# First MoE's first layer of an attention and two-MoE kernel: from fp32r pairs to scaled fp16 pairs, with TensorE's order in the attention stage fixed to the order of the code

## The chip, the cores and the metric

One core of a Trainium2 chip runs the whole program. The metric is the device time of one execution in microseconds (us), the median over runs.

## What is computed

Causal attention over 4 batches x 8 heads x 576 tokens x 64 dims with a bias from a running sum, then two MoE layers without routing, each `x @ w_in`, a gate, and `@ w_out`, over 2304 tokens (512 wide, 2048 inside). The weights come as float64, 8 bytes a number.

```python
bias = -(cum[:, :, :, None] - cum[:, :, None, :])           # cum: running sum of max(s, 0)
scores = where(causal, -1e9, scale * q @ k.T + minimum(bias, 0.0))
attn = exp(scores - scores.max(-1)); attn = attn / (attn.sum(-1) + 1e-9)
x = (attn @ v) as [2304, 512]
h = x @ w_in;  g = h * tanh(log1p(exp(h)));  x = g @ w_out          # first MoE
h = x @ w2_in; g = h / (1 + exp(-1.702 * h)); out = g @ w2_out      # second MoE
```

## The kernel before

**Attention.** It is cut into `steps` (26 a batch, 104 in all): one step is 128 query rows of one to four heads (64 rows of two heads in the last tile of a batch). `tick` emits one step: `do_qk` (tile `s` in PSUM: scores, then a mask matmul), `do_max` (VectorE adds the bias row `ck` and takes the maximum, tile `P`), `do_exp` (ScalarE), and for the batches 1 to 3 `do_hilo` (the probabilities as an fp16 pair, tile `hl`) and a transposing DMA on SP's queue (tile `pt`). `do_av` of a step (tile `o`) is emitted `LAG` ticks later, `emit_tile` (tile `xt`, turned into the unit's `xh`) `EDEL` ticks after a tile's last one. In batch 0 TensorE itself transposes (`early_pt`, tile `pt<-P`, copied to `p`) and nothing of attention is in fp16. Each step needs transposed keys and queries, `kt`/`kw` and `qt`/`qw`, from `kraw` and `qraw`, which POOL's queue loads and ScalarE doubles (`twice`).

**First MoE, first layer.** Tokens go in nine units of 256 (`U`). For each unit `first_layer` runs over 16 blocks of 128 columns of `w_in`; a block is 12 matmuls of 128x256 (`l1_mm`: four blocks of 128 rows, three products each of the pairs high x high, high x low, low x high; tile `h`). After each block `slot_a` emits the ticks that the next units' tokens need, so that attention and `h` are interleaved block by block; this is done for units 0 to 6. Units 7 and 8 run after the last tick, 24 matmuls a block (tile `acc`). ScalarE copies `h` to `hs`, and SP's queue writes it to `h_d`.

**Weights.** `fetch_w` loads one block of `w_in` (512 KB, tile `wst`). ScalarE scales the upper words (`turn_words`), VectorE shifts the lower words and joins them (`turn_join`), ScalarE rounds to the high part and GpSimd subtracts for the low part (`turn_parts`, or all of it in `turn_w`); the result is tile `w`, `[128, 2, 512]` fp32r, 16 of them for the whole first MoE. Five blocks are turned in the start section, the others by `bg_a`.

**What sets the order.** Each engine executes its instructions in one fixed order. In the start section (`nc.mode = "strict"`, up to step 5) that is the order of emission on every engine. Behind it a scheduler chooses the order, from dependencies and a model of durations (`nc.mode = "after"` only says that nothing goes ahead of the start section). `held` keeps an instruction behind the last scores emitted.

Of the kernel before, what the change touches and what calls it, by code (L numbers as in the profile page):

```python
# [19 lines left out]
VTOP = 16384.0  # L20
PH = 3
# [4 lines left out]
MA = 5  # L26
MBB = 2
# [4 lines left out]
HLB = 3  # L32
PB = 2
XTB = 2
PTB = 5
WAH = 3
NP0 = 5
FROM = 7
# [13 lines left out]
LAG = 4  # L52


class Line:
# [4 lines left out]
    def __init__(self, nc, tie):  # L60
        self.nc, self.tie, self.mode, self.last = nc, tie, None, {}
# [7 lines left out]
class Lane:  # L69
# [3 lines left out]
    def __getattr__(self, op):  # L73
# [4 lines left out]
        def run(*a, **kw):  # L78
# [14 lines left out]
def attention_moe_moe_kernel(  # L93
# [81 lines left out]


# [131 lines left out]

    vsc, vmx = {}, {}
# [3 lines left out]
    def vscale_load(b):  # L313
        flat = v[b].rearrange("h t d -> (h t d)").rearrange("(p n) -> p n", p=128)
        vmx[b] = m = sm_p.tile([128, VC + 1], F32, tag="vm", name="vm")
        for c in range(VC):
            t = tmp_pair(F32, "vl")[:, 0:VW]
# [6 lines left out]
    def vscale_set(b):  # L324
# [11 lines left out]
        nc.vector.tensor_scalar(out=t[:, 1:2], in0=t[:, 0:1], scalar1=PSC, scalar2=None, op0=ALU.mult)  # L336
# [273 lines left out]
    def norm_tile(x):  # L610
# [4 lines left out]
        nc.vector.tensor_scalar(out=rs, in0=su, scalar1=1e-9, scalar2=vsc[x["b"]][:, 1:2], op0=ALU.add, op1=ALU.mult)  # L615
        nc.vector.reciprocal(rs, rs)
        nc.gpsimd.tensor_tensor(out=ts["x"], in0=ts["x"], in1=rs.to_broadcast([128, nu, D]), op=ALU.mult)

    def emit_tile(x):
        b, i, n = x["b"], x["i"], x["n"]  # L620
# [6 lines left out]
        pv = ps[:, 0:KC * n].rearrange("p (c t) -> p c t", c=KC)  # L627
        t0 = b * S + 128 * i
        done = 0
        while done < n:  # L630
            u, off = divmod(t0 + done, U)
            m = min(n - done, U - off)
            if u not in xunit:
                xunit[u] = xh_a.tile([128, 2, KC, U], F32R, tag="xh", name="xh")
# [3 lines left out]
            nc.scalar.activation(out=hi, in_=src, func=AF.Copy)  # L638
            nc.vector.tensor_tensor(out=xu[:, 1, :, off:off + m], in0=src, in1=hi, op=ALU.subtract)
# [10 lines left out]
    def queue_prep(gi):  # L650
# [13 lines left out]
        items = items + vs  # L664
        if b + 1 < B and (i, g) in VSTEP:
# [67 lines left out]
    I32 = mybir.dt.int32  # L733
# [8 lines left out]
    def fetch_w(stage, lay, m, kind):  # L742
        if stage:
            rt = stage.tile([128, 1024], F32, tag="wst", name="wst", bufs=NRAW)
        else:
            rt = (wa_p if m < NF - 1 else mo_a).tile([128, 1024], F32, tag="w" if m < NF - 1 else "hs", name="wst")
# [17 lines left out]
    def turn_w(pool, lay, m, kind):  # L764
        t = pool.tile([128, 2, DM], F32R, tag="w", name="w")
        (win_t if kind == "in" else wout_t)[lay, m] = t
        r = fetched.pop((lay, m, kind))
        th, tl_ = t[:, 0, :], t[:, 1, :]
        if not wide:
            nc.scalar.activation(out=th, in_=r, func=AF.Copy)  # L770
            nc.vector.tensor_tensor(out=tl_, in0=r, in1=th, op=ALU.subtract)
            return
        zi, yi = r[:, :, 0], r[:, :, 1]
        y = yi.bitcast(F32)
        sided = lay == 0 and kind == "in"
        if sided:
# [695 lines left out]
```

## Time and profile before

| | us |
|---|---|
| median of 3 runs | 1000.26 (1000.24 to 1002.7) |
| the profiled execution | 1001.29 |
| its span, first to last instruction | 999.3 |
| TensorE matmul busy | 968.8 (97%) |
| VectorE busy | 676.8 (68%) |
| ScalarE busy | 554.3 (55%) |
| GpSimd busy | 289.1 (29%) |

The profiled execution lies 1.0 us above the median. PE is TensorE's matmuls, PEld its weight loads, which overlap them; DVE is VectorE, ACT ScalarE, POOL GpSimd, SP the engine that issues most DMAs. Busy times of matmuls are unions of modelled intervals, so a busy PE is not always one at its peak. Stages by the trace: start section to 36 us, batch 0 of attention to 121, batches 1 to 3 to 392, units 7 and 8 of the first layer to 440, the first MoE's second layer to about 640, the second MoE from there. All engine instructions carry line 79, that of the recording helper; the tiles tell them apart.

### The profile page before, as it was taken

What the parts mean: (1) busy time and instruction counts of PE and PEld (TensorE: products, weight loads), DVE (VectorE), ACT (ScalarE), POOL (GpSimd) and SP (SyncE); (2) the same over time, 40 slices, a digit from 0 to 9 for tenths busy, and PEclk for the clock granted to TensorE, in tenths of its full rate; (3) what the DMA queues carried; (4) which work ended last, traced back from release to release, by engine and by line L of the source; (5) the groups of instructions that cost most, each with busy time, mean ns of one, the idle gap of its engine ahead of it and who ended that gap; (6) DMA issues with size and microseconds to landing.
All of it is one profiled execution on the core that took longest, in us unless ns stands there. A gap on an engine that the chain in (4) does not pass through costs nothing.

```text
span 999.3 us, 20234 instructions
## 1 busy us (share of the span) xinstructions
PE 968.8 (97%) x7974; PEld 863.0 (86%) x7974; DVE 676.8 (68%) x1363; ACT 554.3 (55%) x1062; POOL 289.1 (29%) x358
## 2 busy tenths in 40 slices
PE   8989998989999999999999999999999999999997
PEld 6868996979889889998888888888888888888886
DVE  6878677774666874788997967985554654653553
ACT  5656577785667874786565845643333433333331
POOL 5636442442144330000000000054342424333341
PEclk9999999999999999999999999999999999999999
DMA  9931688996689977899995653400100100000000
GB/s 257 342 88 40 186 192 166 178 239 149 157 167 223 191 144 188 308 330 357 380 308 181 233 187 107 127 1 16 49 22 1 44 23 1 22 22 1 22 13 32
DMA packets 157262, 142.26 MB, mean 142 GB/s; under 512 B 90000, under 2 KB 126352, under 8 KB 157168
## 3 DMA queue, kind: packets, MB, share of 16 engines
q1 hardware_dynamic: 150240, 122.22, 43.9%
q0 software_dynamic: 6928, 18.75, 6.9%
q8 instruction: 63, 1.03, 0.4%
q14 instruction: 31, 0.25, 0.1%
HBM read 89.09 MB, written 32.58 MB: 122 GB/s over the span
## 4 chain that ended last, share of the span: by engine, by line
PE 83%; DMA 5%; DVE 4%; issue 2%; ACT 1%; POOL 0%; SPq 0%; DVEq 0%; POOLq 0%; ACTq 0%
PE h L79 31%; PE acc L79 25%; PE p L79 16%; PE s L79 5%; PE o L79 3%; DMA pt<-hl 3%; PE kt L79 1%; PE qt L79 1%; DMA qraw<-in_q_dram 1%; PE pt L79 1%; DMA vraw<-in_v_dram 1%; DVE w2l L79 1%; PE xt L79 0%; DVE P L79 0%; DMA vl<-in_v_dram 0%
## 5 line engine op out<-in xcount | busy, mean ns | idle before, releaser
L79 PE MATMUL h<-x,w2i 128*128 128x256 f16 x1728 | 199.8, 273 | 0.9 <-DVE z L79 0.9
L79 PE MATMUL h<-xh,w 128*128 128x256 f32 x1344 | 189.7, 290 | 1.7 <-POOL w L79 0.9
L79 PEld LDWEIGHTS <-w2i 128*128 128x128 f16 x1728 | 169.0, 98 | 20.7 <-issue 1.1
L79 PE MATMUL acc<-gh,w 128*128 128x512 f32 (+1 forms) x640 | 181.7, 369 | 0.0
L79 PEld LDWEIGHTS h<-xh,w 128*128 128x128 f32 x1344 | 169.1, 192 | 4.1 <-ACT w L79 1.5
L79 PE MATMUL p<-w2h,gl 128*128 128x256 f16 x504 | 136.1, 273 | 0.5 <-DVE gl L79 0.5
L79 PE MATMUL p<-w2l,gh 128*128 128x256 f16 x504 | 136.1, 273 | 0.0
L79 PEld LDWEIGHTS acc<-gh,w 128*128 128x128 f32 x640 | 116.1, 189 | 20.6
L79 PE MATMUL p<-w2h,gh 128*128 128x256 f16 x504 | 133.5, 273 | 0.2 <-DVE e L79 0.2
L79 PE MATMUL acc<-gl,w 128*128 128x512 f32 (+1 forms) x320 | 117.9, 368 | 0.0
L79 POOL TENSOR_TENSOR s<-z 128x256 f32<-128x256 f32 x72 | 54.8, 783 | 216.9 <-DVE z L79 213.3
L79 DVE TENSOR_TENSOR gl<-z,gh 128x1024 fp32r<-128x1024 f32 (+1 forms) x72 | 94.4, 1313 | 26.8 <-ACT gh L79 26.1
L79 ACT ACTIVATE sg<-h,spx 128x512 f32<-128x512 f32 x72 | 49.0, 680 | 110.5 <-PE h L79 110.5
L79 PEld LDWEIGHTS <-gh 128*128 128x128 f16 x1008 | 98.6, 98 | 11.7 <-issue 0.3
L79 DVE SCALAR_TENSOR_TENSOR z<-h,sg 128x512 f32<-128x512 f32 x72 | 49.5, 687 | 72.3 <-ACT sg L79 72.3
L79 ACT ACTIVATE P<-P,mx 128x384 f32<-128x384 f32 (+4 forms) x128 | 76.5, 599 | 34.8 <-DVE mx L79 33.1
L79 DVE TENSOR_TENSOR gl<-s,gh 128x1024 f16<-128x1024 f32 x36 | 44.3, 1232 | 64.3 <-ACT gh L79 64.3
L79 DVE CUSTOM_DVE_ANT_0 P<-s,ck 128x384 f32<-128x384 f32 (+4 forms) x128 | 61.6, 497 | 34.2 <-PE s L79 26.8
L79 ACT ACTIVATE gh<-z 128x1024 fp32r<-128x1024 f32 (+1 forms) x72 | 67.9, 947 | 28.5 <-DVE z L79 25.4
L79 ACT ACTIVATE gh<-s 128x1024 f16<-128x1024 f32 x36 | 38.0, 1057 | 81.3 <-POOL s L79 81.3
L79 PE MATMUL s<-kw,qw 128*128 128x288 f32 (+4 forms) x352 | 78.5, 333 | 3.1 <-DVE mx L79 1.8
L79 DVE SCALAR_TENSOR_TENSOR wst<-wst 128x512 int32<-128x512 int32 x96 | 70.9, 755 | 2.8 <-ACT wst L79 2.5
(146 smaller groups left out, 1635.1 us busy)
## 6 DMA issues: line engine op xcount, KB each, us to landing
h_d<-hs SPq DMA_DIRECT2D x36, 512.0 KB, 4.6
hg<-h_d SPq DMA_DIRECT2D x36, 512.0 KB, 6.2
wst<-in_moe_w_in_dram SPq DMA_DIRECT2D x32, 512.0 KB, 7.2
wst<-in_moe_w_out_dram SPq DMA_DIRECT2D x32, 512.0 KB, 6.1
x_d<-x SPq DMA_DIRECT2D x18, 256.0 KB, 3.4
out_dram<-o SPq DMA_DIRECT2D x9, 512.0 KB, 2.8
kraw<-in_k_dram POOLq DMA_DIRECT2D x32, 128.0 KB, 4.7
w_d<-w2y SPq DMA_DIRECT2D x16, 256.0 KB, 5.1
```

The source lines that it names most:

```text
L79: r = f(*a, **kw)
```

## The change

1. **fp16 pairs.** `w` and `xh` become fp16 pairs, each scaled by a power of two. A `w` tile now holds a pair of blocks (`[128, 2, 2, 512]` fp16), eight in all. A pair of blocks has one scale, from row sums of absolute values (`pair_sum` on ScalarE, which accumulates) brought across partitions by a matmul with `ones` (`over_rows`, tile `bd`, 2 to 10 columns). The low part is made by VectorE for the first block of a pair and by GpSimd, in two instructions, for the second. Batch 0 gets scales of its own for the units 0 to 2 (`v_peak`, ten reductions over `v`, and `x_scale`); the other batches keep the scale that their `v` already had.
2. **Eviction with a scale.** `evict` multiplies `h` by `ev`, the inverse of both scales; a unit that holds tokens of two classes (units 2, 4 and 6) takes two instructions a bank instead of one.
3. **Stages.** The weights' conversion is cut into `pair_words`, `pair_join`, `pair_sum`, `pair_col`, `pair_scale`, `pair_parts`. Two pairs (four blocks) are turned in the start section, the others by `pairs_to`, a few blocks ahead of their use.
4. **Order.** `nc.pe = True` from the end of the start section up to the last attention step: each TensorE instruction is tied behind the one emitted before it. The other engines keep the scheduler.
5. **Buffers.** `LAG` 4 to 5, `PTB` (tiles `pt`) 5 to 7, `HLB` (tiles `hl`) 3 to 4; `MA`/`MBB` 5/2 to 2/5; `hs` in the attention stage and `vl` move from `mo_a` to the weights' pool, where eight of 16 buffers are free of weights now.

```diff
-HLB = 3
+HLB = 4
-PTB = 5
+PTB = 7
-LAG = 4
+LAG = 5
...
-            if i is not None and line.mode:
+            if i is not None and (line.mode or (line.pe and self.name == "tensor")):
                 if self.name in line.last:
                     line.tie(i, line.last[self.name])
-                if line.mode == "strict":
+                if line.mode == "strict" or (line.pe and self.name == "tensor"):
                     line.last[self.name] = i
...
+    def to_scale(t, src, tiny, top):
+        nc.vector.tensor_scalar(out=t, in0=src, scalar1=tiny, scalar2=1.0 / top, op0=ALU.max, op1=ALU.mult)
+        nc.vector.reciprocal(t, t)
+        pow2(t)
+
+    def over_rows(cols, n):
+        ps = ps_s.tile([128, 512], F32, tag="s", name="bd")
+        nc.tensor.matmul(out=ps[:, 0:n], lhsT=ones, rhs=cols, start=True, stop=True, skip_group_check=True)
+        return ps[:, 0:n]
...
-                xunit[u] = xh_a.tile([128, 2, KC, U], F32R, tag="xh", name="xh")
+                xunit[u] = xh_a.tile([128, 2, KC, U], F16, tag="xh", name="xh")
...
+    def pair_sum(p):
+        wsm[p] = ws = sm_p.tile([128, 2], F32, tag="wsm", name="wsm")
+        for e in range(2):
...
+            lut(junk, y, AF.Abs, accum_out=ws[:, e:e + 1])
...
+    def pair_scale(p):
+        ps = over_rows(wmx.pop(p), 2)
...
+        nc.vector.tensor_reduce(out=k, in_=ps, axis=mybir.AxisListType.X, op=ALU.max)
+        to_scale(k, k, TINY, WTOP1)
+        nc.vector.reciprocal(isw[:, p:p + 1], k)
+
+    def pair_parts(p):
+        k = wkp.pop(p)[:, 0:1]
+        win_t[p] = t = wa_p.tile([128, 2, 2, DM], F16, tag="w", name="w")
+        for e in range(2):
...
+            nc.scalar.activation(out=hi, in_=y, func=AF.Copy, scale=k)
+            if e:
+                nc.gpsimd.tensor_scalar(out=y, in0=y, scalar1=k, scalar2=None, op0=ALU.mult)
+                nc.gpsimd.tensor_tensor(out=lo, in0=y, in1=hi, op=ALU.subtract)
+            else:
+                nc.vector.scalar_tensor_tensor(out=lo, in0=y, scalar=k, in1=hi, op0=ALU.mult, op1=ALU.subtract)
...
+    nc.pe = True
     nxt[0] = avn[0] = 6
...
-    bg_a()
-    bg_a()
+    pairs_to(4, 2)
     queue_prep(NE)
     while prep_q:
         pop_prep(1)
-        bg_a()
+        pairs_to(wq[0], wq[1] + 1 if wq[1] < 3 else wq[1])
...
+    def evict(o, ps, p, t0, t1, n):
+        ov, pv = (x.rearrange("p (d t) -> p d t", d=n) for x in (o, ps))
+        for a, z, k in x_class(t0, t1):
+            e = ev_need(k)[:, p:p + 1]
...
+            nc.scalar.activation(
+                out=ov[:, :, a - t0:z - t0], in_=pv[:, :, a - t0:z - t0], func=AF.Copy, scale=e
+            )
...
-                    while wq and (0, min(NF - 1, m + 2 * e + d + WAH)) not in win_t:
-                        bg_a()
+                    p = (m + 2 * e) // 2
+                    pairs_to(p + 4 + d, p + 2 + d)
...
     while attn_left():
         tick()
+    nc.pe = False
```

How TensorE's instructions stand behind the start section's last warm-up matmuls, before the change: `s` is the first step behind the start section, `h` the first unit, and a row's last factor counts equal instructions in a row.

```order
L79 MATMUL h<-xh,w 128x256 x64
L79 MATMUL kt<-ident,kraw 128x128 x8
L79 MATMUL qt<-ident,qraw 128x128 x4
L79 MATMUL kt<-ident,kraw 128x128 x4
L79 MATMUL h<-xh,w 128x256 x34
L79 MATMUL s<-kw_548,qw 128x384 x2
```

And with the change, up to the same step (of the pair of rows for `w` and `h`, which stands 12 times, one is shown):

```order
L77 MATMUL kt<-ident,kraw 128x128 x4
L77 LDWEIGHTS ones
L77 MATMUL bd<-wmx,ones 128x2
L77 MATMUL kt<-ident,kraw 128x128 x4
L77 MATMUL qt<-ident,qraw 128x128 x4
L77 LDWEIGHTS w
L77 MATMUL h<-xh,w 128x256
L77 MATMUL s<-kw_599,qw 128x384 x2
```

Before the change 98 `h` matmuls stand ahead of that step and 34 more between it and the next one; with the change 12 stand ahead of each. By the first step of batch 1 the count of `h` matmuls ahead is about the same, 218 before and 204 with the change.

VectorE's instructions at the same place, between the last `xh` of the start section and the first bias row (`ISA P,mx`) behind it, before the change (`wst` are weights, `vm` is the maximum of batch 1's `v`):

```order
L79 TENSOR_SCALAR wst<-wst 128x512 x6
L79 SCALAR_TENSOR_TENSOR wst<-wst 128x512 x6
L79 TENSOR_TENSOR kw_548<-kt,kw_548 64x4x128
L79 TENSOR_REDUCE vm<-vl 128x1
L79 SCALAR_TENSOR_TENSOR qw<-qt,qw 128x4x128
L79 TENSOR_REDUCE vm<-vl 128x1 x2
L79 ISA P,mx<-s,ck_207 128x384
```

With the change (`vm_106` is batch 0's `v`, `wk` and `isw` a pair's scale; rows that repeat are left out):

```order
L77 SCALAR_TENSOR_TENSOR w<-wst,wk,w 128x512
L77 TENSOR_SCALAR wst<-wst 128x512 x4
L77 TENSOR_REDUCE vm_106<-v 128x1
L77 SCALAR_TENSOR_TENSOR wst<-wst 128x512 x4
L77 TENSOR_TENSOR kw_599<-kt,kw_599 64x4x128
L77 CAST wmx<-wsm 128x2
L77 TENSOR_REDUCE wk<-bd 128x1
L77 TENSOR_SCALAR wk<-wk 128x1
L77 RECIPROCAL isw<-wk 128x1
L77 SCALAR_TENSOR_TENSOR qw<-qt,qw 128x4x128
L77 ISA P,mx<-s,ck_212 128x384
```

Fewer weights are turned here, and between them and the keys stand the small instructions of the scales; the weights that are left are turned between later steps.

## Rows read from the trace of the kernel before

**Rows 1.** Page, part 1: busy time, share of span, instructions
```profile
PE 968.8 (97%) x7974; PEld 863.0 (86%) x7974; DVE 676.8 (68%) x1363; ACT 554.3 (55%) x1062; POOL 289.1 (29%) x358
```

**Rows 2.** Windows: stretch, length, busy us (count) of each engine, clock, DMA
```profile
0.00:36.00 36.00, 30.95 (x221) 25.22 (x222) 23.87 (x51) 18.02 (x53) 15.22 (x29) 0.95 0.99 284
36.00:60.00 24.00, 20.13 (x156) 18.51 (x155) 18.80 (x25) 15.65 (x34) 17.26 (x18) 1.00 0.84 262
60.00:121.00 61.00, 58.09 (x490) 51.46 (x490) 48.06 (x126) 38.21 (x94) 29.80 (x38) 1.00 0.31 83
121.00:392.00 271.00, 259.70 (x2520) 236.81 (x2518) 190.05 (x526) 196.65 (x500) 92.07 (x124) 0.99 0.85 180
392.00:440.00 48.00, 48.00 (x395) 47.53 (x393) 33.53 (x57) 34.56 (x54) 0.61 (x1) 1.00 0.90 309
```

**Rows 3.** Groups of instructions, PE, whole span: busy us, mean ns, idle before
```profile
L79 PE MATMUL h<-xh,w 128*128 128x256 f32 x1344 | 189.7, 290 | 1.7 <-POOL w L79 0.9 <-ACT w L79 0.8
...
L79 PE MATMUL acc<-xh,w 128*128 128x256 f32 x384 | 46.9, 284 | 0.0
```

**Rows 4.** The same groups, 121 to 392 us
```profile
L79 PE MATMUL h<-xh,w 128*128 128x256 f32 x1103 | 156.0, 290 | 0.0
```

**Rows 5.** Groups of weight loads, whole span
```profile
L79 PEld LDWEIGHTS h<-xh,w 128*128 128x128 f32 x1344 | 169.1, 192 | 4.1 <-ACT w L79 1.5 <-POOL w L79 1.1 <-DVE xh L79 0.2
L79 PEld LDWEIGHTS <-w2i 128*128 128x128 f16 x1728 | 169.0, 98 | 20.7 <-issue 1.1
```

**Rows 6.** Chain that ended last: start, us, what
```profile
238.81 4.39 PE h L79 x36
...
662.63 2.62 PE h L79 x24
```

**Rows 7.** Timeline of PE, 36 to 61 us: start, us, instruction, idle before
```profile
35.83 8.29 PE L79 MATMUL h<-xh,w 128*128 128x256 f32 x64
...
52.10 0.62 PE L79 MATMUL s<-kw,qw 128*128 128x384 f32 x2 [1.20 <-DVE kw L79]
...
60.95 0.60 PE L79 MATMUL s<-kw,qw 128*128 128x384 f32 x2
```

**Rows 8.** Waits of PE, 121 to 392 us: total, times, longest
```profile
PE o L79 <- DMA pt<-hl: 7.1, 6, 2.7
PE s L79 <- DVE mx L79: 1.8, 4, 0.7
...
PE qt L79 <- DVE qw L79: 0.2, 1, 0.2
```

**Rows 9.** Windows around the longest of these waits
```profile
156.00:164.00 8.00, 4.17 (x39) 2.94 (x38) 6.78 (x16) 6.43 (x18) 2.77 (x3) 1.00 1.01 187
...
216.00:224.00 8.00, 4.05 (x46) 3.17 (x41) 5.17 (x15) 7.14 (x22) 3.42 (x5) 0.99 1.21 225
```

**Rows 10.** Groups of VectorE, 0 to 130 us
```profile
L79 DVE SCALAR_TENSOR_TENSOR wst<-wst 128x512 int32<-128x512 int32 x16 | 17.2, 1101 | 0.5 <-ACT wst L79 0.5
...
L79 DVE TENSOR_TENSOR x<-o,rs 128x256 f32<-128x256 f32 x8 | 3.4, 422 | 1.4 <-PE o L79 1.0
...
L79 DVE TENSOR_SCALAR vs<-vs 128x1 f32<-128x1 f32 x2 | 0.3, 144 | 0.0
```

**Rows 11.** Groups of VectorE, 392 to 640 us
```profile
L79 DVE SCALAR_TENSOR_TENSOR wst<-wst 128x512 int32<-128x512 int32 x80 | 53.7, 686 | 2.3 <-ACT wst L79 2.0
```

**Rows 12.** Groups of GpSimd and ScalarE, 0 to 130 us
```profile
L79 POOL TENSOR_TENSOR w<-wst,w 128x512 fp32r<-128x512 f32 x16 | 21.6, 1360 | 24.3 <-ACT w L79 23.8 <-POOL ck L79 0.3
...
L79 ACT ACTIVATE hs<-h 128x512 f32<-128x512 f32 x11 | 6.5, 590 | 5.4 <-PE h L79 4.6 <-issue 0.8
...
L79 ACT ACTIVATION_READ_ACCUMULATOR P<-P,mx 128x1 f32 x25 | 4.7, 189 | 0.0
```

**Rows 13.** Transposing DMAs, all: from issue to landing
```profile
L79 SPq DMA_TRANSPOSE pt<-hl x78: 1209/1253/4089, 127.1 to 387.9; - x78
...
DMA to landing us min/median/max: 2.7/3.8/9.0
```

More of the change, by code (lines that the diff above doesn't have):

```diff
@@ L25 @@
 VB = 12
-MA = 5
-MBB = 2
+MA = 2
+MBB = 5
 NRAW = 4
@@ L335, in vscale_set @@
         nc.vector.reciprocal(t[:, 0:1], t[:, 0:1])
[L336 removed]
+        pow2(t[:, 0:1])
+        ev_table(b, t)
     LK = S // 128 * 128
@@ L762, in fetch_w, with to_f32 @@
         fetched[lay, m, kind] = r
[L764 to L772, printed above, removed]
+    def to_f32(r, first):
         zi, yi = r[:, :, 0], r[:, :, 1]
         y = yi.bitcast(F32)
-        sided = lay == 0 and kind == "in"
-        if sided:
+        if first:
             held(lut(y, y, AF.Prelu, scale=2.0 ** -112, alpha=-(2.0 ** 32)))
@@ L781, in turn_w @@
         nc.vector.scalar_tensor_tensor(
-            out=yi if sided else zi, in0=yi, scalar=3, in1=zi, op0=ALU.logical_shift_left, op1=ALU.bitwise_or
+            out=yi if first else zi, in0=yi, scalar=3, in1=zi, op0=ALU.logical_shift_left, op1=ALU.bitwise_or
         )
-        if not sided:
+        if not first:
             nc.vector.scalar_tensor_tensor(
@@ L814, in mm3, with pair_b, turn_w @@
+    def pair_b(p):
+        pair_scale(p)
+        pair_parts(p)
+    def turn_w(pool, lay, m, kind):
+        t = pool.tile([128, 2, DM], F32R, tag="w", name="w")
+        wout_t[lay, m] = t
+        r = fetched.pop((lay, m, kind))
+        th, tl_ = t[:, 0, :], t[:, 1, :]
+        y = to_f32(r, False) if wide else r
+        nc.scalar.activation(out=th, in_=y, func=AF.Copy)
+        nc.vector.tensor_tensor(out=tl_, in0=y, in1=th, op=ALU.subtract)
     def mm3(outp, hi_w, lo_w, hi_x, lo_x, start, stop):
@@ L827, in attention_moe_moe_kernel @@
     nxt = [0]
-    wq = list(range(NP0, NF))
+    wq = [0, 0]
     fq = list(range(NF))
@@ L833, in fetch_a, with pairs_to @@
             fetch_w(None, 0, fq.pop(0), "in")
-    def bg_a():
-        if wq:
-            m = wq.pop(0)
-            turn_w(wa_p, 0, m, "in")
-            if m >= FROM:
-                fetch_a()
+    def pairs_to(pa, pb):
+        for k, f, n in ((0, pair_a, pa), (1, pair_b, pb)):
+            while wq[k] < min(n, NF // 2):
+                if not k:
+                    f(wq[k])
+                    pair_col(wq[k])
+                else:
+                    f(wq[k])
+                wq[k] += 1
     pt_p = st_t.enter_context(tc.tile_pool(name="pt", bufs=PTB, reuse_waits="tile"))
@@ L874, in attention_moe_moe_kernel @@
         v_load(i_, g, nc.sync)
-    for _ in range(UP):
+    while len(fq) > NF - UP:
         fetch_a()
@@ L892, in attention_moe_moe_kernel @@
     warm(12)
-    turn_words(0)
+    pair_words(0)
+    for g in range(2):
+        v_peak(0, g)
     score(2)
     early_turn(1, 1)
+    early_pt(steps[1])
+    pair_join(0)
+    early_av(steps[0])
+    score(3)
     load_group(0, 2, 0, False)
@@ L904, in attention_moe_moe_kernel @@
         )
-    early_pt(steps[1])
-    turn_join(0)
-    early_av(steps[0])
-    turn_parts(0)
-    turn_words(1)
-    score(3)
     early_pt(steps[2])
     early_av(steps[1])
-    turn_join(1)
-    turn_parts(1)
-    emit_tile(steps[1])
-    turn_words(2)
+    pair_sum(0)
+    for g in range(2):
+        v_peak(1, g)
+    emit_tile_turn(steps[1])
+    x_scale("u0", 2)
+    emit_tile_parts(steps[1])
     score(4)
+    pair_col(0)
     early_pt(steps[3])
     early_av(steps[2])
-    turn_join(2)
+    pair_scale(0)
+    pair_words(1)
     score(5)
-    turn_parts(2)
-    turn_words(3)
+    pair_parts(0)
+    pair_join(1)
     early_pt(steps[4])
```

159 lines of the change are left out of this document (114 added, 45 removed).

## The prediction

> **What bounds the kernel now.** The page's first part comes first: TensorE's matmuls cover 97% of the span, VectorE is next with 68% [rows 1]. An average over stages does not say what each of them waits for, so the windows come second [rows 2]. The reader is to compare the PE column with the length of each stretch: from 392 to 440 us there is no gap at all, from 121 to 392 us 11.3 of 271 us are idle, from 36 to 121 us 6.8 of 85, and in the start section 5.0 of 36. So nearly everywhere a shorter matmul shortens the kernel by what it saves, as long as the order of the work around it stays as tight. Third, the groups of matmuls and the chain give the price of one: 384 fp32r matmuls of 128x256 in an unbroken stream are busy for 46.9 us, 122.1 ns each [rows 3], and inside the attention stage the chain passes through 36 of them in 4.39 us, 121.9 ns each [rows 6]. The second MoE runs the same shape in fp16, and there the chain passes through 24 of them in 2.62 us, 109.2 ns each [rows 6]. Fourth, the timeline behind the start section: 64 `h` matmuls run from 35.8 to 44.1 us while the keys are turned, the next step's scores follow only at 52.1 us, when VectorE has the last `kw`, and the step after that at 60.95 us [rows 7]. Last, the waits: of TensorE's waits after 121 us the transposing DMAs are the largest, 7.1 us in six [rows 8], most of them in two windows with about 4 us of idle time each [rows 9].
>
> **The matmuls.** A change of 122.1 to 109.2 ns is 12.9 ns. There are 1344 matmuls in the units 0 to 6 [rows 3], 1103 of them after 121 us [rows 4], so 241 before, and 384 in the units 7 and 8. That makes -14.2 us in the stretch from 121 to 392, -3.1 us before it and -5.0 us from 392 to 440. The last is safest: PE has no idle time there, and VectorE and ScalarE work 33.5 and 34.6 of 48 us [rows 2], so that 43 us are still enough for them. What goes along with the difference is the weight load, of which each matmul has one: 192 ns for 128x128 in fp32r and 98 ns in fp16 [rows 5], the one longer, the other shorter than a matmul's turn.
>
> **The cover that goes.** Ahead of the second step behind the start section stand 132 `h` matmuls now, 24 with the change; 132 x 122.1 ns = 16.1 us of the 24 us between 36 and 60, in which PE idles 3.9 us [rows 2]. The first of these steps can hardly come earlier: it waits for VectorE, which turns six blocks there now and four then, two shifts and two joins less, but with three reductions, a low part and a dozen small instructions of the scales more. So some 108 matmuls x 109.2 ns = 11.8 us move to between the steps of 60 to 121 us, where PE has 2.9 us to spare. Against that stands the second step, which now waits behind 34 `h` matmuls and the weights they need; without them it comes perhaps 2 us earlier. With half of the 2.9 us filled, 11.8 - 2 - 1.5 = 8.3, so +8 us. If the gaps take everything it is 0.
>
> VectorE's own load bounds this from above. Up to batch 1 it gets ten reductions over `v` (nearest row 128x256, 422 ns: 4.2 us), eight low parts (between the join's 686 ns alone and 1101 ns here: 5.5 to 8.8 us, [rows 10, 11]) and about 73 instructions on a few columns (144 ns: 10.5 us, [rows 10]), 20 to 23 us in all. From 36 to 121 us it is busy for 18.8 + 48.1 = 66.9 of 85 us [rows 2]. The start section takes about 4 us of the addition, so at least 16 come here, 83 in all. Filled to the last microsecond the stage would not grow; at nine tenths, a choice for a chain that goes from engine to engine, 83/0.9 = 92 makes it 7 us longer, close to the 8 from TensorE's side. If both limits bite one after the other it is about +16. The join's two prices, 1101 ns while GpSimd subtracts and 686 ns after 392 us, where GpSimd hardly works, show that the two engines get in each other's way. The Trainium skill ("SBUF — State Buffer", section "SBUF: two separate sides") says why: a VectorE instruction with two SBUF inputs and a GpSimd instruction take one port pair in turns. By that rule the eight low parts cost the upper of the two prices, 8.8 us.
>
> **The order and LAG.** From 121 to 392 us there are 78 steps, one transposing DMA each [rows 13], so 3.5 us a step on average. With `LAG` at 5 a product with `v` stands one step further behind its DMA. The longest of the six waits is 2.7 us [rows 8], so an average step would remove all 7.1; but in the windows where they lie the steps without `h` follow each other faster, so I take half, -3.5 us, between 0 and -7.1. The fixed order can cost: TensorE can no longer run `h` early where scores are late. Its waits for VectorE there are 4.0 us in five rows, the first and the last of which are shown [rows 8], 0.05 us a step, in an order that was also fixed, only chosen by the scheduler; I take 0 for it, and 16 us (0.2 us a step) as its bound.
>
> **Small additions.** Eleven matmuls for `bd` go into TensorE's line; each takes between a weight load's 98 ns [rows 5] and the 284 ns of a whole matmul of 256 columns [rows 3], so 1.1 to 3.1 us, +1.5. The sums of absolute values, 16 times about 590 + 189 ns [rows 12] = 12.5 us of ScalarE, and 24 more evictions of 189 to 590 ns (4.5 to 14 us) lie in ScalarE's idle time: 18.0 us of the start section and 74 us after 121 us [rows 2]. Without that cover they would be 17 to 27 us; I take 0. GpSimd's 16 subtractions of 1360 ns [rows 12] become eight, with eight scalings that are no longer than those. `vl` and `hs` in the weights' pool get eight free buffers, so no transfer has to wait longer; the exchange of `MA` and `MBB` leaves seven buffers after 392 us, where PE does not wait. Both cost nothing there.
>
> **Sum.** Against the profiled execution's 1001.3 us: -14.2 - 3.1 - 5.0 + 8 - 3.5 + 1.5 = -16.3, so 985.0; the median of the runs is 1.0 us under the profiled one, so **984 us**.
>
> **Rivals.**
> - *The cover is not missed.* The gaps between the steps of batch 0 take the moved matmuls, and all of the 7.1 us goes: 984 - 8 - 3.5 = 972.5. For it speaks VectorE's 18.1 idle us; against it that those lie spread out behind other engines. Chance 0.15.
> - *Batch 0 goes to VectorE.* The stage grows by 16 us instead of 8, and `LAG` gives back nothing: 984 + 8 + 3.5 = 995.5. For it speaks the 83 of 85 us of work above. Chance 0.10.
> - *Slower: each step stalls a little.* In the fixed order TensorE stands at a score, a `kt` or a `bd` that VectorE or ScalarE has not released, with the next `h` queued behind it. The price is 78 times the loss a step. At 0.25 us it eats the 16.3 us and the 3.5 of `LAG`; at 0.3 it is 23.4, so 984 + 3.5 + 23.4 = 1011. Speaking for it: VectorE and ScalarE are busy 70 and 73% there [rows 2], and a step passes TensorE, VectorE, ScalarE and a DMA in turn. Against: 0.05 us a step now. Chance 0.08.
> - *The matmuls do not get shorter.* If the 122.1 ns came from the columns' pace and not from the weights, 22.3 us would be gone: 984 + 22.3 = 1006. The 98 and 192 ns speak against it. [...] Chance 0.02.
>
> **How the numbers follow.** The forecast has 0.65, with its own range from 976 to 992. A measurement of this kernel can tell about 0.3%, 3 us. Faster than 997.3 are the forecast, the first rival and most of the second (0.07): 0.87. Slower are most of the third (0.06) and the fourth: 0.08; 0.05 is left for no change. The range reaches from the first rival with a little more, 969, to 998, above the second; outside are the last two rivals and the edges.
>
> **What would show it.** Right: the matmuls `h<-xh,w` and `acc<-xh,w` at 109 ns in the chain, loads of `w` near 98 ns; the first score behind the start section near 52 us with idle PE ahead of it; batch 1 starting at 124 to 128 us; units 7 and 8 in 43 us; fewer waits on `pt`. Wrong: if batch 1 starts before 119 us the cover was not missed; if waits of TensorE for VectorE pass 20 us after 121 us, the fixed order stalls; if `h` stays at 122 ns, the type does not matter; an idle PE between 440 and 640 us would be something none of this expects.

## The result, and the profile after

The changed kernel takes **1015.42 us** (median of 4 runs, 1012.87 to 1018.89) against 1001.48 of the kernel before in the same job: a ratio of 1.0135, 95% interval 1.0093 to 1.0178. It is slower by 1.3%; forecast were 984 us, and 969 to 998 as the range. The profiled execution took 1016.07 us, its span is 1014.2.

The page's busy times, to be read beside [rows 1]:

```profile
PE 957.0 (94%) x7985; PEld 826.9 (82%) x7985; DVE 689.8 (68%) x1460; ACT 572.8 (56%) x1118; POOL 293.6 (29%) x360
```

TensorE is busy for 12 us less, and the span is 15 us longer, so 27 us of idle time are new. The windows say where (columns as in [rows 2]; the last attention step ends at 411 us now, units 7 and 8 at 454):

```profile
0.00:36.00 36.00, 27.98 (x195) 21.72 (x195) 23.36 (x61) 18.37 (x56) 12.69 (x29) 0.95 0.99 286
36.00:60.00 24.00, 13.26 (x64) 10.26 (x65) 19.96 (x47) 15.65 (x36) 15.05 (x15) 0.60 0.60 181
60.00:121.00 61.00, 56.56 (x460) 48.47 (x459) 49.59 (x156) 40.47 (x95) 33.91 (x36) 0.93 0.23 69
121.00:411.00 290.00, 263.57 (x2676) 224.03 (x2675) 202.55 (x560) 210.96 (x545) 97.03 (x132) 0.96 0.83 179
411.00:454.00 43.00, 43.00 (x394) 38.55 (x392) 29.02 (x48) 29.92 (x46) 0.00 (x0) 1.00 0.84 292
```

Between 36 and 60 us TensorE stands still for 10.7 of 24 us, and its granted clock averages 0.60, so most of that stretch lies at the lower of its two levels (1.2 GHz instead of 2.4). The stretch to the last attention step has 26 us without a matmul, where [rows 2] had 11, and a clock of 0.96 instead of 0.99. Units 7 and 8 fill their 43 us without a gap, as they filled 48.

The matmuls did get shorter. From the groups and the chain of after:

```profile
L77 PE MATMUL h<-xh,w 128*128 128x256 f16 x1344 | 173.9, 284 | 11.6 <-ACT xh L77 9.2 <-DVE xh L77 2.4
L77 PE MATMUL acc<-xh,w 128*128 128x256 f16 x384 | 42.2, 273 | 0.0
L77 PEld LDWEIGHTS <-w 128*128 128x128 f16 x1728 | 169.4, 101 | 36.8 <-issue 13.9
...
408.86 2.62 PE h L77 x24
```

384 `acc` in an unbroken stream take 42.2 us, 109.9 ns each, where [rows 3] had 46.9; 24 `h` of the chain take 2.62 us, as the second MoE's did in [rows 6]. The first row has the new cost: TensorE idled 11.6 us ahead of `h`, for ScalarE and VectorE to convert `xh`; ahead of `h` of before it was 1.7 us, for weights [rows 3].

The waits of TensorE from 121 to 411 us (total, times, longest) have changed their kind:

```profile
PE h L77 <- ACT xh L77: 9.2, 6, 2.7
PE qt L77 <- ACT qraw L77: 3.7, 1, 3.7
PE kt L77 <- issue: 2.5, 1, 2.5
PE o L77 <- DMA pt<-hl: 2.5, 3, 1.3
PE h L77 <- DVE xh L77: 2.4, 6, 0.6
```

The wait on `pt` fell from 7.1 us in [rows 8] to 2.5. What is new stands at the borders of units, as the timeline of PE at one of them shows (start, us, instruction, idle time before it):

```profile
233.83 0.49 PE L77 MATMUL xt<-ident,x 128*128 128x128 f32 x3
236.60 0.37 PE L77 MATMUL h<-xh,w 128*128 128x256 f16 x1 [2.27 <-ACT xh L77]
237.22 0.59 PE L77 MATMUL h<-xh,w 128*128 128x256 f16 x2 [0.25 <-DVE xh L77]
```

In the code a unit's `h` follows the `xt` of its last tile. In between lie the eviction, the rounding and the low part on two other engines, and an order that is fixed puts nothing there.

The same view behind the start section, beside [rows 7]:

```profile
43.26 1.11 PE L77 MATMUL kt<-ident,kraw 128*128 128x128 f32 x4 [1.27 <-ACT kraw L77]
49.37 0.18 PE L77 MATMUL bd<-wmx,ones 128*128 128x2 bf16 x1 [4.99 <-DVE wmx L77]
...
52.05 2.65 PE L77 MATMUL h<-xh,w 128*128 128x256 f16 x12
54.53 0.61 PE L77 MATMUL s<-kw,qw 128*128 128x384 f32 x2
...
59.44 1.11 PE L77 MATMUL kt<-ident,kraw 128*128 128x128 f32 x4 [4.23 <-ACT kraw L77]
```

TensorE waits 5 us for the first `bd` behind the start section, with keys queued behind it, and then 4.2 us for `kraw`. Twelve `h` take 2.65 us there, twice their price, in the window whose granted clock averages 0.60.

Cut at the start of batch 1, the windows are, in after:

```profile
36.00:135.00 99.00, 82.53 (x652) 69.84 (x653) 79.08 (x230) 65.18 (x152) 52.69 (x56) 0.86 0.38 112
135.00:411.00 276.00, 250.87 (x2547) 212.93 (x2545) 193.03 (x534) 201.89 (x524) 93.29 (x127) 0.96 0.84 179
```

And in before (its batches 1 to 3 are in [rows 2]):

```profile
36.00:121.00 85.00, 78.22 (x646) 69.97 (x645) 66.86 (x150) 53.85 (x126) 47.06 (x55) 1.00 0.46 134
```

Up to batch 1 TensorE idles 16.5 us instead of 6.8 and is busy for 4.3 us more, with shorter matmuls, at a mean clock of 0.86 instead of 1.00. Behind it 25 us are idle instead of 11. Part of the first difference is older than the window: the last warm-up matmul of the start section ends at 42.0 us in after and at 36.0 in before.

So the change splits into three stages, whose ends can be read for every kernel: where batch 1 starts (its first mask matmul, the 37th of the program), where units 7 and 8 end (the last `acc<-xh,w`), and the end. The stages are worked out from the timeline of PE, `h` counts the matmuls `h<-xh,w` ahead of batch 1 (the 218 and 204 of the section on the change stand ahead of the last step of batch 0), us:

```
                              batch 1 at   h   to end of units 7, 8   rest
before                          120.9    241         318.0           560.4
after                           135.4    216         318.2           560.6
forecast, mid of 124 to 128     126                  296             560
e2  before, order fixed         129.0    228         335.2           559.7
e1  free order, LAG 5           135.8    218         309.9           560.6
e4  fixed from unit 1 on        139.3    216         313.5           562.2
e6  fixed, LAG 4                137.0    228         328.5           560.6
e9  fixed, LAG 5, one step more 136.0    216         314.0           562.2
e16 fixed, LAG 5, constant w    132.7    216         324.3           560.6
e3  free order, LAG 4           137.8    229         300.5           562.2
e5    and all scales constant   125.6    229         305.2           562.5
e11   and scales of w constant  127.0    229         304.2           562.3
e13   e11 with the sums         127.9    229         308.6           560.6
e14   without the sums alone    133.3    229         304.0           560.6
e10   conversions do not wait   134.6    229         312.0           562.2
e15   scales by two pairs       137.5    261         306.9           562.2
e12   v's peaks on ScalarE      138.9    229         310.5           562.2
e8    low parts on GpSimd       147.7    262         310.7           560.5
e7    more warm-up matmuls      138.7    229         309.6           565.3
```

The forecast's 296 is 318.0 - 14.2 - 5.0 - 3.5 and the rest of the small additions. Against it the start is 9 us late and the middle 22 us too long.

Each row is read from one execution, and executions of one kernel differ by as much as 10 us (e3: 997.87 to 1007.98) and more; where in the program they differ is not known. So a difference of a few us between two rows is not shown by them; what several kernels repeat is firmer. A kernel with fewer `h` ahead of batch 1 has as many more in its middle, 0.11 to 0.12 us each.

### The profile page after: what moved, and what is told of

It reads as the page before. It is cut to its first block, busy times and chain, and to the rows that moved or that the text cites. A ratio compares the mean times of both kernels' runs of the same rounds, so it can differ in the third digit from the quotient of the medians.

```text
span 1014.2 us, 20398 instructions
## 1 busy us (share of the span) xinstructions
PE 957.0 (94%) x7985; PEld 826.9 (82%) x7985; DVE 689.8 (68%) x1460; ACT 572.8 (56%) x1118; POOL 293.6 (29%) x360
## 4 chain that ended last, share of the span: by engine, by line
PE 58%; DVE 1%; ACT 1%; DMA 0%; issue 0%; DVEq 0%; SPq 0%
PE acc L77 24%; PE h L77 18%; PE p L77 16%; DMA pt<-hl 0%; DVE w2d L77 0%; DVE w2l L77 0%; DVE o L77 0%; ACT L77 0%; ACT w2h L77 0%; DVE f L77 0%; DVE gl L77 0%; PE xt L77 0%; DVE hl L77 0%; ACT hs L77 0%; ACT sg L77 0%
## 5 line engine op out<-in xcount | busy, mean ns | idle before, releaser
L77 PEld LDWEIGHTS <-w 128*128 128x128 f16 x1728 | 169.4, 101 | 36.8 <-issue 13.9
L77 PE MATMUL h<-xh,w 128*128 128x256 f16 x1344 | 173.9, 284 | 11.6 <-ACT xh L77 9.2
L77 PE MATMUL p<-w2h,gl 128*128 128x256 f16 x504 | 135.8, 273 | 1.0 <-DVE gl L77 1.0
L77 PE MATMUL s<-kw,qw 128*128 128x288 f32 (+4 forms) x352 | 82.1, 347 | 2.2 <-DVE xh L77 1.2
L77 ACT ACTIVATE wst<-wst 128x512 f32<-128x512 f32 x80 | 53.7, 686 | 38.1 <-DMA wst<-in_moe_w_out_dram 24.9
```

The source lines that it names most:

```text
L77: r = f(*a, **kw)
```

## Experiments

All ratios are to the kernel before, run on the same chip in the same job.

**The order alone, undone and put on its own.** Two theories: the fixed order makes TensorE idle (order), or the instructions added to VectorE and ScalarE in batch 0 do (work).

e1, the changed kernel with the order left to the scheduler:

```diff
-    nc.pe = True
+    nc.pe = False
```

> The changed kernel with TensorE's order left to the scheduler again (the tie of order is off behind the start section), all else as changed. Theory order: the loss comes from the fixed order, which leaves TensorE idle where the keys are turned and lowers its clock. Then the first block of h stands ahead of the keys again, the first score of batch 1 comes at 120 to 126 us instead of 135, attention ends before 388 us and the time is 978 to 992 us. Theory work: the loss comes from the added instructions of the scales on VectorE and ScalarE in batch 0, whatever TensorE's order is. Then batch 1 still starts after 131 us and the time is above 1005 us.

1011.36 us, ratio 1.0076 (1.0041 to 1.0111), as theory work had it. Batch 1 starts no earlier, so undoing the order alone does not bring the start back. The middle of the profiled execution is 8 us shorter; by all executions the gain is 4 to 6 us, and the interval overlaps that of the changed kernel (1.0093 to 1.0178), so that a cost of the order by itself with `LAG` at 5 is likely, but not shown.

e2, the kernel before with the same tie on TensorE:

```diff
-            if i is not None and line.mode:
+            if i is not None and (line.mode or (line.pe and self.name == "tensor")):
...
-                if line.mode == "strict":
+                if line.mode == "strict" or (line.pe and self.name == "tensor"):
...
     nc.mode = "after"
+    nc.pe = True
...
         tick()
+    nc.pe = False
     switch_set("mish")
```

> The kernel before, fp32r and all its buffers, with the tie of TensorE's order alone added. Theory order: it loses what the changed kernel lost and has no shorter matmuls to set against it, so 1020 to 1040 us, with stretches at the lower clock between 36 and 120 us. Theory work: the order costs little by itself, 998 to 1006 us.

1029.43 us, ratio 1.0228 (1.0184 to 1.0271), as theory order had it; the clock from 36 to 60 us is 0.57. On the kernel before the fixed order by itself makes the start 8 us late and the middle 17 us longer. 1.6 us of the 17 are 13 `h` that moved there, which leaves 15.6 / 78 steps = 0.20 us a step.

e3, e1 with the old `LAG`:

```diff
-LAG = 5
+LAG = 4
```

> As e1_free, with LAG back at 4 (the larger pools stay). If a step more behind the transposing DMA is worth the 3.5 us of the forecast, it is 2 to 5 us slower than e1_free; if the scheduler finds other work for these waits anyway, it is within 2 us.

1002.16 us, ratio 0.9969 (0.9942 to 0.9997). Neither reading had that: it is 9 us faster than e1, and the intervals lie apart. Behind batch 1's start it needs 300.5 us, 17.5 less than before: four fifths of the 22 us that were forecast for that stage. In batch 0 it is as late as the others.

e4, the order fixed only from unit 1 on:

```diff
-    nc.pe = True
...
     for u in range(NU - UE):
+        nc.pe = u > 0
```

> The changed kernel with the order fixed from the second unit on only; the scheduler orders the first unit with batch 0. Theory order, with the larger share at the start: batch 1 starts at 120 to 126 us, the stalls at the units' first blocks after it stay, and the time is 995 to 1004 us. If the start is not what loses, it stays above 1008 us.

1015.21 us, ratio 1.0092 (1.0057 to 1.0126). The start is not earlier with a free order there.

**LAG under the fixed order.** e6, the changed kernel with:

```diff
-LAG = 5
+LAG = 4
```

> The changed kernel with LAG at 4 alone, TensorE's order still fixed. Theory 'LAG 5 makes a unit's input late': it costs the same with the order fixed, 8 us in batches 1 to 3, so 1007 us, 1.004 of the kernel before, and the gaps of 2 to 3 us ahead of a unit's first h disappear. Theory 'it is the fixed order alone': no change by LAG, 1.013; with the products nearer to their DMAs the waits for pt may even grow by 5 us, 1.018.

1027.99 us, ratio 1.0244 (1.0215 to 1.0272). Both theories were wrong in their numbers, the second came nearer. Its waits of TensorE from 137 to 423 us, with the unit borders' wait as in after and the one on `pt` five times that of after:

```profile
PE o L77 <- DMA pt<-hl: 13.6, 10, 3.8
PE h L77 <- ACT xh L77: 9.7, 5, 3.0
PE h L77 <- DVE xh L77: 5.6, 5, 4.0
```

With the order left free, the same `LAG` (e3, 138 to 390 us) has:

```profile
PE o L77 <- DMA pt<-hl: 5.3, 7, 1.2
...
PE h L77 <- ACT xh L77: 1.3, 2, 0.7
```

And with the order free and `LAG` at 5 (e1, 136 to 400 us):

```profile
PE o L77 <- DMA pt<-hl: 10.5, 10, 2.4
```

And two stretches side by side, e6 first, then e3:

```profile
137.00:423.00 286.00, 250.95 (x2531) 212.60 (x2531) 192.44 (x534) 201.57 (x522) 92.84 (x127) 0.96 0.80 173
```

```profile
138.00:390.00 252.00, 240.95 (x2496) 206.87 (x2497) 189.15 (x530) 201.65 (x524) 92.97 (x125) 1.00 0.90 192
```

The same work takes 34 us longer in the fixed order: 24 us more idle time, and 10 us more busy time. 35 matmuls more are some 4 us of that; the clock, 0.96 instead of 1.00, goes with the rest. `LAG` at 5 takes 11.1 us of the waits on `pt` away (13.6 to 2.5), and the stage is 10.3 us shorter (328.5 to 318.2). In a free order no such gain is seen: the waits on `pt` are 10.5 us with `LAG` 5 (e1) and 5.3 with 4 (e3). The middle of e1 is 309.9, and the ten kernels with a free order and `LAG` 4 lie between 300.5 and 312.0.

**The units' borders.** e9, one step more between the tile that completes a unit and its first `h`:

```diff
         while tok_done[0] < (u + 1) * U:
             tick()
+        if u:
+            tick()
```

> The changed kernel (order fixed, LAG 5) with one step more between the tile that completes a unit's input and the unit's first h, for the units 1 to 6; nothing is left out. Theory 'the fixed order stalls at the units' borders': the gaps of 2 to 2.7 us behind xt at 234, 267 and 308 us go, and the half-clock stretches behind the first two of them with them, so 5 to 10 us less, 1.003 to 1.008 of the kernel before. Rival 'the fixed order stalls wherever something is late': the idle time moves to the o, kt and qt of the step put in, and the time stays at 1.011 or above.

1014.75 us, ratio 1.0110 (1.0083 to 1.0136): the rival's number, the intervals of this and of after overlap. The waits of TensorE, 121 to 411 us:

```profile
PE kt L77 <- DVE mx L77: 4.1, 4, 1.4
PE qt L77 <- ACT qraw L77: 3.9, 2, 2.8
PE o L77 <- DMA pt<-hl: 3.2, 2, 2.6
...
PE h L77 <- ACT xh L77: 1.9, 2, 1.7
```

The wait of `h` for ScalarE's `xh` fell from 9.2 to 1.9 us, and `kt` and `o` wait instead. The place of the stall was right, the gain was not: here the next thing that was late took most of it over.

**What makes the start late.** All kernels from here on stand on e3, but for e16.

e5, constants instead of all scales (no `v_peak`, no sums, no `bd`, no `wk`, no products for `ev`):

```diff
...
-        wkp[p] = k = sm_p.tile([128, 2], F32, tag="wk", name="wk")
...
+        wkp[p] = kcon
...
```

> The version with free order and LAG at 4, with the scales of the first layer taken as constants: no reductions over v, no sums of absolute values, no bd, no small instructions for the scales; the fp16 pairs, the low parts and the evictions with a scale stay. What is left out is the finding of the scales, so the output is rounded differently. Theory 'VectorE's added work sets batch 0': VectorE is busy for 83 of the 100 us from 36 us to batch 1 there, against 66.9 of 85 before; some 13 us of that are the scales, so batch 1 starts at 125 to 129 us instead of 137.8, and the time is 9 to 13 us shorter, 0.985 to 0.988 of the kernel before. Theory 'the matmuls that stood ahead of batch 0 are what is missing': batch 1 still starts at 134 us or later, and the time stays at 0.993 or above.

998.01 us, ratio 0.9938 (0.9913 to 0.9962). Batch 1 starts 12.2 us earlier, as the first theory had it; the ratio lies above the 0.985 to 0.988 that it gave, since 4.7 us are lost again behind it (305.2 against 300.5).

e7, more warm-up matmuls:

```diff
+    warm(12)
...
-    warm(8)
+    warm(32)
...
+        hold(8)
         pairs_to(wq[0], wq[1] + 1 if wq[1] < 3 else wq[1])
```

> The version with free order and LAG at 4, with 36 matmuls more of 128x256 on a zero tile in the start section and 8 behind each preparation up to step 9, so that TensorE is not idle there; nothing is left out. Theory 'the half clock is a cause': the granted clock stays at 1.0 from 36 to 105 us, where it is 0.79 to 0.91 over the stretches of 20 us now, and batch 1 starts 4 to 8 us earlier. Theory 'VectorE's added work': the clock rises, and batch 1 starts at 137 us or later, since TensorE is waited for by nobody there.

1013.64 us, ratio 1.0091 (1.0061 to 1.0121). The first two stages' windows, e3 above, e7 below:

```profile
36.00:60.00 24.00, 17.62 (x111) 14.21 (x111) 19.75 (x48) 15.17 (x35) 16.38 (x16) 0.79 0.59 184
60.00:121.00 61.00, 53.36 (x398) 43.90 (x399) 52.44 (x160) 40.65 (x98) 30.35 (x34) 0.92 0.22 65
```

```profile
36.00:60.00 24.00, 20.88 (x185) 18.45 (x186) 18.37 (x47) 14.85 (x33) 18.09 (x16) 1.00 0.45 141
60.00:121.00 61.00, 53.12 (x405) 44.62 (x403) 51.36 (x161) 41.15 (x99) 31.18 (x35) 0.92 0.27 81
```

The clock stayed up from 36 to 60 us and batch 1 came no earlier, at 138.7. So the low clock ahead of 60 us is not shown to be a cause; the 74 more matmuls that held it up stand in TensorE's line too, and what they cost is not separated. Behind 60 us the clock fell all the same, so that stretch is not tested.

e8, both low parts of a pair on GpSimd:

```diff
-            if e:
+            if True:
                 nc.gpsimd.tensor_scalar(out=y, in0=y, scalar1=k, scalar2=None, op0=ALU.mult)
```

> The version with free order and LAG at 4, with both low parts of a pair on GpSimd, as all of them were before, instead of every second on VectorE. Theory 'VectorE's added work': the eight low parts leave it, 5.5 to 8.8 us, and batch 1 starts 4 to 8 us earlier, 0.990 to 0.994 of the kernel before. Against it: GpSimd takes two instructions of 1.6 to 2.6 us for each low part, so that pairs come 4 us later and the h behind them wait; then nothing is won or 5 us are lost.

1017.78 us, ratio 1.0142 (1.0113 to 1.0171); batch 1 10 us later, 3.6 of them for 33 `h` more ahead of it. Nothing was won, as the case against had it, and more was lost than its 5 us. In after one scaling takes GpSimd 1957 ns on average and one subtraction 1332. That the weights come later by that is not shown: in e8 TensorE waits only 0.6 us for `w` from 36 us to batch 1.

```profile
L77 POOL TENSOR_SCALAR wst<-wst,wk 128x512 f32<-128x512 f32 x8 | 15.7, 1957 | 34.6 <-DVE w L77 19.4 <-ACT w L77 15.1
...
L77 POOL TENSOR_TENSOR w<-wst,w 128x512 f16<-128x512 f32 x8 | 10.7, 1332 | 0.6
```

e12, the reductions over `v` moved from VectorE to ScalarE:

```diff
-        peak(vm0[:n, 2 * i + g:2 * i + g + 1], vt[0, i, g][:n].rearrange("p h d -> p (h d)"))
+        lut(vj[:n], vt[0, i, g][:n].rearrange("p h d -> p (h d)"), AF.Abs, accum_out=vm1[:n, 2 * i + g:2 * i + g + 1])
...
+        nc.vector.tensor_copy(vm0[:, 0:2 * ni], vm1[:, 0:2 * ni])
```

> The version with free order and LAG at 4, with the ten reductions over v on ScalarE, as sums of absolute values, instead of VectorE; the scale of x becomes smaller by the ratio of sum and peak. 'VectorE's load': 4.2 us leave it, ScalarE with 66 of 102 us busy takes ten times 0.6 us; batch 1 starts 2 to 4 us earlier than 137.8 us and the time is 0.993 to 0.995 of the kernel before. 'The chain': ten instructions in ScalarE's line ahead of the evictions, nothing won, 0.996 or above.

1010.78 us, ratio 1.0070 (1.0044 to 1.0096), batch 1 at 138.9. Taking 4 us of work off VectorE and putting it on ScalarE gave nothing. VectorE's load as a sum is not all that sets the start; whether ScalarE's new work took the gain back, the run can't tell.

**Which part of the scales.** e11, constants for the scales of the weights alone (no sums, casts, `bd`, reductions; `x_scale` stays):

```diff
-            lut(junk, y, AF.Abs, accum_out=ws[:, e:e + 1])
...
-        nc.vector.tensor_copy(t, wsm.pop(p))
...
-        to_scale(k, k, TINY, WTOP1)
-        nc.vector.reciprocal(isw[:, p:p + 1], k)
+        wkp[p] = kcon
...
+    nc.gpsimd.memset(isw, 1.0 / 256.0)
```

> The version with free order and LAG at 4 with constant scales for the weights alone; those of x in batch 0 are still found from v. Left out: the sums of absolute values (12.5 us of ScalarE), eight bd and some 48 small instructions of VectorE; it keeps ten reductions and 24 products for the evictions. 'The weights' chain': nearly all of the 12.2 us, batch 1 at 125 to 128 us. 'The work by its length on VectorE': 48 x 144 ns = 6.9 of some 15 us go, about half, so batch 1 at 131 to 133 us.

996.49 us, ratio 0.9936 (0.9915 to 0.9958). Batch 1 at 127.0: in a free order the scales of the weights cost 10.8 of the 12.2 us. In the three free-order kernels without the chain that finds them (e5, e11 and e13 below) batch 1 starts at 125.6 to 127.9; in the six that leave nothing out (e1, e3, e7, e8, e12, e15) at 135.8 to 147.7, the latest with 33 `h` more ahead of it.

e10, where the scales are found, but nothing but the evictions waits for them:

```diff
-                k_ = f"u{u}"
-                k_ = sx[k_][:, 0:1]
+                k_ = kcon[:, 0:1]
...
-        k = wkp.pop(p)[:, 0:1]
+        wkp.pop(p)
+        k = kcon[:, 0:1]
```

> The version with free order and LAG at 4, in which the scales are found as before but the conversions of batch 0 and of the weights take a constant instead, so that nothing waits for a scale but the evictions; the constants make the output another one. It tells what in the scales costs the 12.2 us by which batch 1 came earlier with constant scales (125.6 instead of 137.8 us). 'VectorE's load': the instructions are all still there, batch 1 starts at 134 us or later. 'The chain from the sums to the low parts': the pairs come earlier, batch 1 starts at 129 us or earlier. In between: both.

1007.26 us, ratio 1.0032 (1.0008 to 1.0056), batch 1 at 134.6: by these executions not waiting gives 3.2 us, and against e11 the weights' instructions by being there cost 7.6.

e13 and e14 put back one half each of what e11 leaves out: e13 the 16 sums on ScalarE (with nobody to use them), e14 the casts, `bd` and small instructions (on a constant). Against e11 and against e3:

```diff
+        ws = sm_p.tile([128, 2], F32, tag="wsm", name="wsm")
...
+            lut(junk, y, AF.Abs, accum_out=ws[:, e:e + 1])
```

```diff
-        wsm[p] = ws = sm_p.tile([128, 2], F32, tag="wsm", name="wsm")
+        wsm[p] = kcon
...
-            lut(junk, y, AF.Abs, accum_out=ws[:, e:e + 1])
...
+    nc.gpsimd.memset(kcon, 1.0)
```

> The version with free order, LAG at 4 and constant scales of the weights, with the 16 sums of absolute values on ScalarE put back; nothing uses them, and the scales of the weights stay left out. 'ScalarE's sums (12.5 us of work) cost the start': batch 1 at 134 us or later, as with all of the scales (137.8). 'VectorE's small instructions and bd cost it': batch 1 at 127 to 129 us, as without (127.0).

> The version with free order and LAG at 4 without the 16 sums on ScalarE; the casts, bd and the small instructions of VectorE stay and work on a constant, and the conversions wait for them. Left out: the sums, so the scales of the weights are those of a constant. 'ScalarE's sums': batch 1 at 127 to 130 us. 'VectorE's small instructions and bd': 134 us or later.

e13: 997.12 us, ratio 0.9941 (0.9918 to 0.9963), batch 1 at 127.9. e14: 999.21 us, ratio 0.9949 (0.9929 to 0.9970), batch 1 at 133.3. By these executions the sums by themselves cost 0.9 us, the chain behind them 6.3, both together 10.8. That the sums alone cost little is plain; the 3.6 us that would come only from the two standing in line are no larger than the differences that one execution each can leave.

e15, one chain for two pairs from pair 2 on (casts and `bd` over four columns, scales in two):

```diff
...
-        ps = over_rows(wmx.pop(p), 2)
+        ps = over_rows(wmx.pop(p)[:, 0:2 * n], 2 * n).rearrange("p (a b) -> p a b", a=n)
...
```

> The version with free order and LAG at 4 with one chain of cast, bd, reduction and scale for two pairs at a time from pair 2 on; nothing is left out. 18 small instructions of VectorE (2.6 us) and three bd less. 'VectorE's small instructions and bd': batch 1 2 to 4 us earlier than 137.8, 0.993 to 0.995 of the kernel before. 'ScalarE's sums': no gain, and pair 2 later by one sum: 0.997 to 1.000.

1010.26 us, ratio 1.0054 (1.0029 to 1.0078). Batch 1 starts at 137.5 with 32 `h` more ahead of it, 3.5 us of work, which is about the gain expected; 6.4 us are lost behind it (306.9 against 300.5).

e16, the changed kernel (order fixed, `LAG` 5) with e11's constant scales, which is e11 with:

```diff
-LAG = 4
+LAG = 5
...
-    nc.pe = False
+    nc.pe = True
```

> The changed kernel as it is (order fixed, LAG 5) with constant scales of the weights, the one part left out. If the start's loss and that of the fixed order stand side by side: batch 1 at 125 to 128 instead of 135.4 us, and 7 to 11 us less in all, 1.003 to 1.006 of the kernel before. If the fixed order only hands the gain on to its own stalls: 1.010 or above.

1016.87 us, ratio 1.0120 (1.0089 to 1.0151). The start is 2.7 us earlier and the middle 6.1 us longer. Under the fixed order the scales' removal gives nothing: the losses do not stand side by side. Together with e1 this says that either one, the fixed order or the scales, is enough to make the start late; only without both (e5, e11, e13) does it come near the forecast's 126.

## Why the prediction was wrong

**What held.** The price of a matmul, 109 ns; units 7 and 8, 42.2 us instead of 46.9 (-4.7, forecast -5.0); the rival by which both types would cost the same falls. The first score behind the start section near 52 us with idle PE ahead: 54.5. Fewer waits on `pt`. The rest of the program, 560 us, did not change.

**The step that failed first: "I take 0 for it".** The forecast carried the small waits of the old order, 0.05 us a step, over to the fixed one. But that order had small waits because the scheduler had put other work where something was late. Tied down, the kernel before lost 0.20 us a step behind batch 0 (e2), the changed one with `LAG` 4 between (328.5 - 312.0) / 78 = 0.21 and (328.5 - 300.5) / 78 = 0.36 (e6 against the free ones): the bound of 16 us, or more. With `LAG` 5, as it was built, it is (318.2 - 309.9) / 78 = 0.11 against e1, 8 of the 22 us by which the middle was too long; undoing order and `LAG` together (e3) gives 17.7. The third rival, TensorE standing at what is late with other work queued behind it, is what happened from 121 to 411 us. Its places were partly others than named: `pt` and a unit's first `h` more than `kt`. In e9 the wait moved on from one of them to others. The forecast's sign for it, more than 20 us of waits for VectorE, did not show: these are 8 us, those for ScalarE 13, in 26 us of idle time.

**LAG, -3.5: the mechanism holds under the fixed order, at another size.** There it removed 11.1 us of waits on `pt` and 10.3 us of time, as it had more to remove than the 7.1 us of before. In the free order it removed none: e1, with `LAG` 5, waits longer on `pt` than e3 and is 9 us slower. Why is open; the scheduler made another order for each. So order and `LAG` together cost 6 to 18 us in the middle (318.2 against 312.0 and 300.5); forecast were -3.5.

**The cover that goes, +8: too small.** Batch 1 started at 135.4 us, with 25 `h` fewer ahead of it, so 14.5 + 25 x 0.109 = 17.2 us late, where +8 - 3.1 and a part of the additions were forecast. The +16 "if both limits bite one after the other" was nearer. Two terms were missing. The sum priced all work at the full clock, and the clock of this stretch fell to 0.86 on average; what that costs by itself is not separated. And `kt`, ahead of which 64 `h` stood before, now waits for `kraw`: from 36 us to batch 1 this is 6.5 us in after, 9.4 in e2 and 6.1 in e11, against 1.0 before.

VectorE's sum did not decide it: it came out as forecast, 79.1 us in after (36 to 135 us) and 83.0 in e3 (36 to 138), against 83. The upper price of its low parts did not come in after. There the 16 joins take 743 ns each on average, not 1101 [rows 10], and the low parts 746:

```profile
L77 DVE SCALAR_TENSOR_TENSOR wst<-wst 128x512 int32<-128x512 int32 x16 | 11.3, 743 | 0.0
...
L77 DVE SCALAR_TENSOR_TENSOR w<-wst,wk,w 128x512 f16<-128x512 f32 x8 | 6.0, 746 | 2.2 <-ACT w L77 2.2
```

The average hides what happened, as the shortest, median and longest of the 16 joins show, before first, then after:

```profile
L79 DVE SCALAR_TENSOR_TENSOR wst<-wst x16: 674/682/5200, 17.8 to 90.9; 128x512 int32<-128x512 int32 x16
```

```profile
L77 DVE SCALAR_TENSOR_TENSOR wst<-wst x16: 677/682/1643, 19.7 to 88.0; 128x512 int32<-128x512 int32 x16
```

The usual join costs 682 ns in both. Four of before and one of after are longer, and each of these ended 0.55 us behind the end of a subtraction of GpSimd; the one of 5200 ns stood behind three of them in a row. That agrees with the rule of the Trainium skill ("SBUF — State Buffer", section "SBUF: two separate sides") that was weighed there, for subtractions, which read two tensors. Beside GpSimd's scalings, which read one and which that section does not except, joins and low parts of after were not longer, 0.68 to 0.75 us; in e3 three of them took 0.9 to 1.1 us.

With a free order, what made the start late is above all the finding of the weights' scales: sum, cast, `bd`, reduction and four small instructions, 10.8 us (e11), most of it the part on VectorE and TensorE (e14). In the changed kernel it is not that alone: without these scales its start is only 2.7 us earlier (e16), and the fixed order by itself made that of the kernel before 8 us late (e2). The forecast had listed these 48 instructions by their length, about 7 us, as work that VectorE's idle time would mostly take in. It did not: in e14 they cost 6.3 us, nearly their whole length. They stand in VectorE's line between the steps, and each pair passes three engines before its `h` may run; what that waiting adds, 3.2 us by e10, is not clear of the differences between executions.

**The middle in the free order.** Even there the forecast's 296 us was not reached: 300.5 at the best, 312.0 at the worst, for edits that lie in batch 0 almost alone. This spread of 11.5 us is as large as most effects looked for. It comes from the order that the scheduler finds, or in part from one execution to the next, which was not separated. So a gain of some us of one version over another (e12, e10, e15 in their total times) says nothing by itself; differences that recur in several kernels do.

**What stays open.** Whether sums and chain cost more together than each alone; how much of the loss in either stage is the lower clock and how much the waits; what the clock behind 60 us costs, since e7 held it up only ahead of that; and what the new sizes of the buffers do, which no run undid.

**A version level with the kernel before.** e3, free order and `LAG` 4 with everything else of the change, has a ratio of 0.9969 (0.9942 to 0.9997), with all of the computation. Of the 17.5 us that it gains behind batch 1's start it pays 16.9 in batch 0. As the best of several versions it is too near to 1 to be called faster; against the changed kernel it gains 1.7%, with intervals apart.

## What to carry to other kernels

Small waits in an order that a scheduler chose are no measure for a fixed one: find what the scheduler moved between, and count that as a wait at every such place. Here, in before, scores, products with `v` or keys and queries stood between a unit's last `xt` and its first `h` at all six borders, and TensorE waited at none; in after nothing stood there, and it waited 0.5 to 2.7 us at each. An option that hides a latency, as `LAG`, must be judged in the order in which it will run; it gave 10 us in the fixed one and cost 9 in the one pair of runs in the free one. And a chain of tiny instructions on engines that are not the bottleneck is not free because these have idle time: here 48 of them, about 7 us by their length, cost 6.3 us of the start in the free order.

## What was not expected of the hardware

TensorE's granted clock: in after it averages 0.60 from 36 to 60 us, where the engine stands still for 45% of the time, and in the windows around the two waits of more than 2 us at the units' borders (234 and 267 us) it is below 1 again:

```profile
225.00:250.00 25.00, 21.07 (x211) 17.34 (x212) 16.88 (x46) 20.02 (x58) 10.70 (x16) 0.86 0.87 202
250.00:275.00 25.00, 21.91 (x197) 18.34 (x196) 12.37 (x25) 11.39 (x27) 3.68 (x5) 0.89 0.63 171
```

The kernel before had 0.96 and 1.00 in the same two windows, with 0.0 and 1.2 us idle. GpSimd's scaling of 128x512 by a column, without a second tensor, took 1957 ns on average (1636 to 2582), 0.6 us more than its subtraction of two tensors of that size; the forecast had set it no higher than that.
